# Weight conversion of the first block reordered: joins ahead of the activation, a word pass inside it, the rest behind the copies

## The chip, the cores and the metric

The kernel runs on one core of a Trainium2 chip. The metric is the device time of one execution in microseconds. TensorE (PE) does the matrix products, VectorE (DVE), ScalarE (ACT) and GpSimd (POOL) the elementwise work, and SyncE (SP) issues the DMAs. Each engine takes its instructions strictly in the order in which the program lists them.

## The reference

Three stages follow each other: an attention with a decaying state over 4 batches, 8 heads, 768 steps and 48 features, then two feed-forward layers over 3072 tokens with 384 features and a hidden width of 2048.

```python
for t in range(S):
    state = alpha[:, :, t, :, None] * state + np.einsum('bhd,bhe->bhde', k[:, :, t], v[:, :, t])
    y[:, :, t] = np.einsum('bhd,bhde->bhe', q[:, :, t], state)
x = y.transpose(0, 2, 1, 3).reshape(B * S, H * D)
h = x @ w_in                                        # layer 1
x = (np.maximum(h, 0.0) + alpha * np.minimum(h, 0.0)) @ w_out
h = x @ w_in2                                       # layer 2
g = np.where(h >= 1, h, np.where(h <= -1, 0.0, (h + 1) ** 2 / 4))
out = g @ w_out2
```

The four weight matrices are float64, everything else float32. The kernel needs them as float32.

## The kernel before, in words

The tokens are cut into 24 attention chunks of 128, and for the layers into 6 blocks of 512 (first layer), then 6 blocks of 512 (second). The hidden width is cut into 16 weight chunks of 128. A **step** is one block with one weight chunk: nine hidden products (`emit_h`, L490), the activation (`emit_act`), and the nine products of the step before into the output (`emit_out1`, L523). Step s of the first block uses weight chunk s.

All order is written out by hand: the kernel lists instructions, and every engine takes its own share of the list in that order. The lists `mids` and `ends` hold the pieces of attention that go into a step, `mids` between the hidden and the output products, `ends` behind the output products.

**Activation in layer 1:** ACT scales the hidden product by the leak (L504), DVE takes the maximum (L508), ACT rounds it to `gh` (L513), POOL forms the rest `gl` (L514).

**Weight conversion.** A weight chunk comes in by seven DMAs (`load_w`, L410 to L414) into a staging tile `wst` of which there are three buffers. Its 64-bit words become float32 in two ACT passes (`words_f32`, L420 and L422, "word passes"), and two DVE passes (`join_f32`, L428 and L431, "the join") into a tile `wf`. Then ACT copies it rounded into `wh` (L468, "weight copy") and POOL forms the rest `wl` (L474, "weight pass"). In the first block, step s joins and splits chunk s+2 and does the word passes of chunk s+3. So the first block carries conversion, attention of the next tokens, and its own products at once.

**Attention in the first block.** From step 2 on a chunk takes three steps. Call them A, B and C. In A, PE transposes a part of the next chunk, DVE clamps it (L197), PE transposes the last part (L205), does the output products of the chunk before (L352, L292) and the next state (L324); ACT copies the result (L374, L378), DVE forms its low part (L379, L381) and the state (L336 to L341), and multiplies (L261). In B come the masked products (L311), a scan (L244) and a multiply (L261), in C a scan (L251) and one more transpose (L267).

**The start.** Four attention chunks (c = 0 to 3) run before the first step, on their own, while the first weight chunks load. In c = 2 and 3 their conversion is woven in. There, L363 copies the part of the result that the matmuls with `sel` (L370) spread, and L374 copies the result into the tile `xs` from which the hidden products read.

Of the kernel before, what the change touches and what calls it, by code (L numbers as in the profile page):

```python
# [7 lines left out]
F32 = mybir.dt.float32  # L8
# [14 lines left out]
def kernel(  # L23
# [15 lines left out]
    NT, DM = out.shape  # L39
    DFF = w_in1.shape[1]  # L40
    P = 128
# [3 lines left out]
    NFC = DFF // P  # L45
# [16 lines left out]
    wpool = main.enter_context(tc.tile_pool(name="wpool", bufs=1))  # L62
# [30 lines left out]
    NC0 = NB2 // C  # L93
    spare = iter([f"w{x}{i}" for i in range(NFC - 1, 0, -1) for x in "lh"])
    own = {}

    def spare_tile(key, shape, name):

        if key not in own:
            own[key] = wpool.tile(shape, F32, tag=next(spare), name=name)  # L100
        return own[key]
# [58 lines left out]
    def v_of(c):  # L160

        if c < NC0:
            return spare_tile(("v", c), [P, H, 64], f"v{c}")
        return vt_b[c % 2][:, 0:H * D].rearrange("t (h d) -> t h d", d=D)
# [10 lines left out]
    def load_v(c, eng):  # L175
        b, t0 = c // CPB, (c % CPB) * C
        eng.dma_start(out=v_of(c)[:, :, 0:D], in_=v[b, :, t0:t0 + C, :].rearrange("h t d -> t h d"))
# [239 lines left out]
    def words_f32(lo, hi, t, nbias, part=None):  # L417

        if part != 1:
            nc.scalar.activation(hi.bitcast(F32), t[:, :, 1].bitcast(F32), AF.Copy, scale=2.0 ** -112)  # L420
        if part != 0:
            nc.scalar.activation(lo, t[:, :, 0], AF.Relu, scale=2.0 ** -29, bias=nbias)  # L422
# [16 lines left out]
    def conv_words(layer, fc, part=None):  # L439
        t = stg[layer, fc]  # L440
        if wide:
            w = t.rearrange("p a (n two) -> p (a n) two", two=2)
            words_f32(w[:, :, 0], w[:, :, 1], w, mhalf, part)

    def conv_join(layer, fc, part=None):
        t = stg[layer, fc]
        if wide:
            w = t.rearrange("p a (n two) -> p (a n) two", two=2)
            if part != 1:
                own["f"] = (spare_tile(("f", fc), [P, 2 * DM], "wf") if layer == 0 and fc < 2 else  # L450
                            p1.tile([P, 2 * DM], F32, tag="wf", name="wf"))
            join_f32(own["f"], w[:, :, 0], w[:, :, 1], part)
            if part != 0:
                stg[layer, fc] = own["f"]
        elif part != 0:
            stg[layer, fc] = t.rearrange("p a f -> p (a f)")
# [9 lines left out]
    def split_hi(layer, fc):  # L466
        hi = wpool.tile([P, 2 * DM], F32R, tag=f"wh{fc}", name=f"wh{fc}")
        nc.scalar.copy(out=hi, in_=stg[layer, fc])  # L468
        wt[layer, fc] = [hi, None]

    def split_lo(layer, fc):
        hi = wt[layer, fc][0]
        lo = wpool.tile([P, 2 * DM], F32R, tag=f"wl{fc}", name=f"wl{fc}")
        nc.gpsimd.tensor_sub(out=lo, in0=stg.pop((layer, fc)), in1=hi.bitcast(F32))  # L474
        wt[layer, fc][1] = lo
# [16 lines left out]
                i += 1  # L492
        return hp

    def emit_act(layer, fc, hp, n, parts=1):
        g = p2.tile([P, n], F32, tag="g", name="g", padded_shape=[P, 512])
        gh = p2.tile([P, n], F32R, tag="gh", name="gh", padded_shape=[P, 512])
        gl = p2.tile([P, n], F32R, tag="gl", name="gl", padded_shape=[P, 512])
        cuts = [[t[:, i * n // parts:(i + 1) * n // parts] for t in (hp, g, gh, gl)] for i in range(parts)]
        for x, y, _, _ in cuts:  # L500
            if layer:
                nc.scalar.activation(y, x, AF.Relu, bias=half, scale=0.5)  # L502
            else:
                nc.scalar.activation(y, x, AF.Copy, scale=malpha[:, fc:fc + 1])  # L504
        for x, y, hi, lo in cuts:
            if layer == 0:

                nc.vector.tensor_max(out=y, in0=x, in1=y)  # L508
            else:
                nc.vector.scalar_tensor_tensor(out=y, in0=y, scalar=1.0, in1=y,  # L510
                                               op0=ALU.min, op1=ALU.mult)
                nc.vector.tensor_max(out=y, in0=x, in1=y)  # L512
            nc.scalar.copy(out=hi, in_=y)  # L513
            (nc.gpsimd if parts == 1 else nc.vector).tensor_sub(out=lo, in0=y, in1=hi.bitcast(F32))  # L514
        return gh, gl
# [44 lines left out]
    def xdst(c):  # L560
        j = chunk_blk[c]
        return x_tile(j), c * C - blk[j][1]

    def fetch(c, i=None):

        if c >= NCH:
            return
        if c < NPE:
            for x in (2, 1, 0) if i is None else (i,):
                at_in_pe(c, x, c < NC0)  # L570
            if not i and NC0 + 1 < c + 2 < NPE:
                load_chunk(c + 2, nc.sync)
            if not i and c == NPE - 1:
                nc.gpsimd.memset(natq[:, :, 4 * D - 32:], 1.0)
                load_blocks(NPE)
            return
        for x in (2, 1, 0) if i is None else (i,):
            at_in(c, x)
        if not i and c + 1 < NCH:
            load_blocks(c + 1)  # L580
# [15 lines left out]
    for c in range(NC0, NCH + 1):  # L596
        n = 3 if c < 2 * NC0 else 4
        s = 2 + 3 * (c - NC0) if c < 2 * NC0 else 2 + 3 * NC0 + 4 * (c - 2 * NC0)
# [22 lines left out]
    def run_slots(where, s):  # L621
        for f in where.pop(s, ()):
            f()

    with tc.manual_schedule():
        steps = [(j, fc) for j in range(len(blk)) for fc in range(NFC)]
        gs = {}
        ops_t = {}

        def w1_load(i):  # L630
            if 0 <= i < NFC:
                load_w(0, i, nc.sync)

        def w1_words(i):
            if 0 <= i < NFC:
                conv_words(0, i)

        def w1_join(i):
            if 0 <= i < NFC:
                conv_join(0, i)  # L640

        def w1_split(i):
            if 0 <= i < NFC:
                split_hi(0, i)
                split_lo(0, i)
# [19 lines left out]
                split_hi(1, i)  # L665
                split_lo(1, i)

        def do_h(s):
            j, fc = steps[s]
            layer, t0, n = blk[j]  # L670
            hp = emit_h(layer, fc, xs_t[j], n)
            gs[s] = emit_act(layer, fc, hp, n, 2 if s == len(steps) - 1 else 1)

        def banks(tags, n):

# [80 lines left out]
        for c in range(NC0):  # L756
            i = c - NC0 + 2
            if c < NC0 - 1:
                at_mul(c + 1, "K2", nc.vector)
                at_mul(c + 1, "Q2", nc.gpsimd)  # L760
            at_within(c)
            if c + 2 < NC0:
                fetch(c + 2, 2)
            if c < NC0 - 1:
                at_kt(c + 1)
            if c + 2 < NC0:
                fetch(c + 2, 1)
                fetch(c + 2, 0)
                at_scan(c + 2, "R")
                at_scan(c + 2, "F")  # L770
            w1_join(i)
            at_out(c, xdst(c), True, (lambda: split_hi(0, i)) if i >= 0 else None)
            if c % 2 == 0:
                load_v(NC0 + c // 2, nc.sync)
            if i >= 0:
                split_lo(0, i)
                w1_load(i + 3)
            w1_words(i + 1)
        mps = ps_h.tile([P, NFC], F32, tag="h", name="mps", padded_shape=[P, 512])
        nc.tensor.transpose(out=mps, in_=ma, identity=ident[0:NFC, 0:NFC])  # L780
        nc.scalar.copy(out=malpha, in_=mps)
# [2 lines left out]
        for s in range(len(steps) + SK):  # L784
            if s < len(steps):
                j, fc = steps[s]
                do_h(s)
            run_slots(mids, s)
            if s < NFC:
                w1_join(fc + 2)  # L790
                w1_load(fc + 5)
            if s >= SK:
                do_out(s - SK)
            run_slots(ends, s)
            if s < NFC:
                w1_split(fc + 2)
                w1_words(fc + 3)
            if s < len(steps):
                if j == n1 - 1 and fc == 0:
                    w2_split(-1)  # L800
                if NFC - 2 <= s < (n1 - 1) * NFC:
                    w2_step(s)
                if n1 - 1 <= j < len(blk) - 1:
                    if fc in (8, 10, 12):
                        split_x2(j + 1, (fc - 8) // 2)
                    if fc in (5, 7, 9):
                        load_x2(j + 1, (fc - 5) // 2)
                i = s - (n1 + 1) * NFC
                if i >= 0 and i % 2 == 0 and i // 2 < NFB * NFL:
                    load_flags(i // 2)  # L810
                if i == 0:
                    flag(malpha, 2, 2 * NCH - 1)
                if 0 <= i - 4 < 2 * NFB * NFL:
                    flag(own["al", (i - 4) // 2], i % 2, i - 4)
# [181 lines left out]
```

## Time and profile before

| what | value |
|---|---|
| median of 3 runs | 958.64 us (952.84, 958.64, 958.99) |
| the profiled execution | 952.87 us, its span 951.1 us |
| PE busy over the span | 909.2 us (96%) |
| DVE busy | 493.6 us (52%) |
| ACT busy | 413.8 us (44%) |
| POOL busy | 389.9 us (41%) |
| read from HBM | 66.66 MB |

The shares are means over the whole span, in which the first 158 us (start and first block) and the rest are of two kinds. A time in brackets in a row of a timeline is what the engine sat idle before that instruction, with what ended it.

### The profile page before, as it was taken

Reading aid. Unit: us, or ns where it says so; the run is one execution under the profiler, and the core shown is the slowest. Engines: PE = TensorE matmul, PEld = TensorE weight load, DVE = VectorE, ACT = ScalarE, POOL = GpSimd, SP = SyncE. Lnnn points to the kernel's source line nnn. Section 1 sums busy time; section 2 is a strip of 40 time slices with the busy share of each in tenths; the row PEclk is TensorE's granted clock in tenths of the full one; section 3 lists DMA queues with packets and bytes.
Section 4 is the critical chain, followed back from the end, with each engine's and each line's share of the span. In section 5 each row is a group of like instructions: output and inputs, shape, how many; then the busy total and the mean of one; then the engine's idle time right before and its main releaser. Section 6 shows DMA issues by size and latency. Waiting matters only on the chain.

```text
span 951.1 us, 17365 instructions
## 1 busy us (share of the span) xinstructions
PE 909.2 (96%) x6955; PEld 773.7 (81%) x6955; DVE 493.6 (52%) x675; ACT 413.8 (44%) x668; POOL 389.9 (41%) x310
## 2 busy tenths in 40 slices
PE   6877888999999999999999999999999999999996
PEld 5766667788788788788778889999999999999995
DVE  6588886756666566574312234434335344344332
ACT  2556555444444443444445533346555333333332
POOL 4255454544445444453357743233323332332331
PEclk9899899999999999999999999999999999999999
DMA  9864762674555554462043220122220100100001
GB/s 165 176 139 122 153 121 65 178 179 119 146 146 148 151 129 112 126 175 63 24 162 122 67 67 1 43 81 61 83 67 1 67 1 1 67 1 1 34 1 37
DMA packets 119896, 85.57 MB, mean 90 GB/s; under 512 B 64752, under 2 KB 105472, under 8 KB 119808
## 3 DMA queue, kind: packets, MB, share of 16 engines
q1 hardware_dynamic: 119808, 84.39, 34.7%
q8 instruction: 56, 0.92, 0.4%
q14 instruction: 32, 0.26, 0.1%
HBM read 66.66 MB, written 15.73 MB: 87 GB/s over the span
## 4 chain that ended last, share of the span: by engine, by line
PE 82%; DVE 6%; DMA 5%; SPq 3%; issue 2%; ACT 1%; DVEq 0%; ACTq 0%
PE hp L490 38%; PE y_oo L523 11%; PE y_yy L534 7%; PE y_oo L534 7%; PE y_o L523 5%; PE y_o L534 3%; PE y_at L534 3%; DVE wf L431 2%; DMA wst<-in_moe_w_in_dram 2%; PE w L352 2%; DMA xs<-x 1%; PE w L292 1%; PE w L324 1%; SPq L410 1%; DVE wf L428 1%
## 5 line engine op out<-in xcount | busy, mean ns | idle before, releaser
L514 POOL TENSOR_TENSOR gl<-g,gh 128x512 fp32r<-128x512 f32 x191 | 257.1, 1346 | 486.6 <-ACT gh L513 406.8
L490 PE MATMUL hp<-xs,wh 128*128 128x512 f32 x1152 | 368.3, 401 | 3.1 <-DMA xs<-x 1.3
L490 PEld LDWEIGHTS hp<-xs,wh 128*128 128x128 f32 x1152 | 212.4, 190 | 43.9 <-issue 2.4
L490 PE MATMUL hp<-xs,wl 128*128 128x512 f32 x576 | 227.6, 395 | 0.0
L513 ACT CAST gh<-g 128x512 fp32r<-128x512 f32 (+1 forms) x193 | 119.3, 618 | 226.8 <-DVE g L512 143.9
L510 DVE SCALAR_TENSOR_TENSOR g<-g 128x512 f32<-128x512 f32 (+1 forms) x97 | 67.7, 697 | 207.7 <-ACT g L502 206.3
L490 PEld LDWEIGHTS hp<-xs,wl 128*128 128x128 f32 x576 | 109.3, 190 | 24.1
L508 DVE TENSOR_TENSOR g<-hp,g 128x512 f32<-128x512 f32 x96 | 66.2, 690 | 113.4 <-ACT g L504 112.6
L504 ACT ACTIVATE g<-hp,malpha 128x512 f32<-128x512 f32 x96 | 65.9, 687 | 122.7 <-PE hp L490 121.9
L502 ACT ACTIVATE g<-hp,half 128x512 f32<-128x512 f32 (+1 forms) x97 | 66.5, 686 | 94.0 <-PE hp L490 93.4
L512 DVE TENSOR_TENSOR g<-hp,g 128x512 f32<-128x512 f32 (+1 forms) x97 | 66.5, 686 | 3.4
L523 PE MATMUL y_oo<-gh,wh 128*128 128x512 f32 x192 | 60.2, 395 | 0.0
L523 PE MATMUL y_oo<-gl,wh 128*128 128x512 f32 x192 | 59.7, 392 | 0.4 <-POOL gl L514 0.4
L523 PE MATMUL y_oo<-gh,wl 128*128 128x512 f32 x192 | 59.6, 392 | 0.0
L474 POOL TENSOR_TENSOR wl<-wf,wh 128x768 fp32r<-128x768 f32 x16 | 32.8, 2050 | 30.0 <-ACT wh L468 30.0
L431 DVE SCALAR_TENSOR_TENSOR wf<-wst,wf 128x768 uint32<-128x768 uint32 x32 | 44.4, 1389 | 0.5
L230 DVE STREAM_TRANSPOSE T<-nat 128x512 f32<-128x512 f32 x42 | 43.3, 1084 | 0.0
L523 PEld LDWEIGHTS y_oo<-gl,wh 128*128 128x128 f32 x192 | 36.0, 188 | 8.5 <-POOL gl L514 0.9
L523 PEld LDWEIGHTS y_oo<-gh,wl 128*128 128x128 f32 x192 | 36.1, 188 | 7.7
L523 PEld LDWEIGHTS y_oo<-gh,wh 128*128 128x128 f32 x192 | 35.6, 188 | 7.3
L379 DVE TENSOR_TENSOR xs<-w,xs 128x384 fp32r<-128x384 f32 x24 | 13.4, 558 | 51.1 <-ACT x L378 47.3
L523 PE MATMUL y_o<-gl,wh 128*128 128x512 f32 x96 | 37.7, 393 | 0.0
(123 smaller groups left out, 1384.8 us busy)
## 6 DMA issues: line engine op xcount, KB each, us to landing
wst<-in_moe_w_out_dram SPq DMA_DIRECT2D x32, 384.0 KB, 4.4
wst<-in_moe_w_in_dram SPq DMA_DIRECT2D x16, 384.0 KB, 4.2
w_d<-wf SPq DMA_DIRECT2D x16, 384.0 KB, 2.7
w<-w_d SPq DMA_DIRECT2D x16, 384.0 KB, 3.0
x_d<-ev SPq DMA_DIRECT2D x18, 256.0 KB, 2.5
x2s<-x_d SPq DMA_DIRECT2D x18, 256.0 KB, 3.5
out_dram<-ev SPq DMA_DIRECT2D x24, 192.0 KB, 2.0
al<-in_alpha_dram SPq DMA_DIRECT2D x12, 384.0 KB, 3.3
```

What stands on the lines that cost most here:

```text
L230: nc.vector.transpose(out=tin(c, i).rearrange("f n (j g) -> f n g j", g=4), in_=natq[:, n].rearrange("j n (g f) -> j n g f", g=4)[:, :, :, ...
L431: nc.vector.scalar_tensor_tensor(out=fu, in0=hi, scalar=0x80000000, in1=fu, op0=ALU.bitwise_and, op1=ALU.bitwise_or)
L490: nc.tensor.matmul(out=hp, lhsT=w[:, p, :], rhs=xs[:, x, p, :], start=(i == 0), stop=(i == 3 * ND - 1))
L502: nc.scalar.activation(y, x, AF.Relu, bias=half, scale=0.5)
L504: nc.scalar.activation(y, x, AF.Copy, scale=malpha[:, fc:fc + 1])
L508: nc.vector.tensor_max(out=y, in0=x, in1=y)
L510: nc.vector.scalar_tensor_tensor(out=y, in0=y, scalar=1.0, in1=y, op0=ALU.min, op1=ALU.mult)
L512: nc.vector.tensor_max(out=y, in0=x, in1=y)
L513: nc.scalar.copy(out=hi, in_=y)
L514: (nc.gpsimd if parts == 1 else nc.vector).tensor_sub(out=lo, in0=y, in1=hi.bitcast(F32))
L523: nc.tensor.matmul(out=ops[d], lhsT=w[:, d * P:(d + 1) * P], rhs=g, start=first, stop=last)
L534: nc.tensor.matmul(out=ops[t], lhsT=g[:, t * P:(t + 1) * P], rhs=w, start=first, stop=last)
```

## The change

In the start, the two transposes of a later chunk (`fetch(c + 2, 1)` and `fetch(c + 2, 0)`) go into the chunk's output, behind L363, and the two join passes are parted: the first stays ahead of the output, the second goes behind it. The weight copy leaves the output, and comes last. The loader's call is no longer under `if i >= 0`, and stands ahead of the word passes.

In the first block, the join goes ahead of the hidden products, the first word pass goes into the activation between L504 and the rounding, the second behind the attention's copies, and the weight copy and weight pass behind it. The joined weights of a chunk go into the place of the next chunk's `wl`, where one tile `wf` served most chunks.

```diff
@@ conv_join
             if part != 1:
-                own["f"] = (spare_tile(("f", fc), [P, 2 * DM], "wf") if layer == 0 and fc < 2 else
+
+                own["f"] = (wpool.tile([P, 2 * DM], F32, tag=f"wl{fc + 1}", name="wf")
+                            if layer == 0 and fc + 1 < NFC else
                             p1.tile([P, 2 * DM], F32, tag="wf", name="wf"))
@@ emit_act
+        if mid:
+            mid()
         for x, y, hi, lo in cuts:
@@ the start, for c in range(NC0), i = c - 2
             if c + 2 < NC0:
-                fetch(c + 2, 1)
-                fetch(c + 2, 0)
                 at_scan(c + 2, "R")
                 at_scan(c + 2, "F")
-            w1_join(i)
-            at_out(c, xdst(c), True, (lambda: split_hi(0, i)) if i >= 0 else None)
+            w1_join(i, 0)
+
+            def mid():
+                if c + 2 < NC0:
+                    fetch(c + 2, 1)
+                    fetch(c + 2, 0)
+
+            at_out(c, xdst(c), True, mid)
             if c % 2 == 0:
                 load_v(NC0 + c // 2, nc.sync)
+            w1_join(i, 1)
+            w1_load(i + 3)
+            w1_words(i + 1)
             if i >= 0:
-                split_lo(0, i)
-                w1_load(i + 3)
-            w1_words(i + 1)
+                w1_split(i)
@@ the steps
                 j, fc = steps[s]
-                do_h(s)
+                if j == 0:
+                    w1_join(fc + 2)
+                    w1_load(fc + 5)
+                do_h(s, (lambda: w1_words(fc + 3, 0)) if j == 0 else None)
             run_slots(mids, s)
-            if s < NFC:
-                w1_join(fc + 2)
-                w1_load(fc + 5)
             if s >= SK:
                 do_out(s - SK)
             run_slots(ends, s)
             if s < NFC:
+                w1_words(fc + 3, 1)
                 w1_split(fc + 2)
-                w1_words(fc + 3)
```

How it moves instructions, at three places. The first is SP's queue in the start; `vt0` and `vt1` are v of attention chunks 4 and 5, a tile `wst_` with its number is one load of a weight chunk. Before, wst_605 is chunk 3:

```order
L177 DMA vt0_98<-in_v_dram 128x8x48
L177 DMA vt1_99<-in_v_dram 128x8x48
L410 DMA wst_605<-in_moe_w_in_dram 48x2x256
L410 DMA wst_605<-in_moe_w_in_dram 48x256
L411 DMA wst_605<-in_moe_w_in_dram 16x3x256
```

With the change, where wst_395 is chunk 1, wst_515 chunk 2 and wst_617 chunk 3:

```order
L177 DMA vt0_98<-in_v_dram 128x8x48
L410 DMA wst_395<-in_moe_w_in_dram 48x2x256
...
L414 DMA wst_395<-in_moe_w_out_dram 128x768
L410 DMA wst_515<-in_moe_w_in_dram 48x2x256
...
L414 DMA wst_515<-in_moe_w_out_dram 128x768
L177 DMA vt1_99<-in_v_dram 128x8x48
L410 DMA wst_617<-in_moe_w_in_dram 48x2x256
```

Two loads of seven DMAs each are new there; the loads of chunks 1 and 2 that stood earlier in the queue (wst_187 and wst_197) stand there still.

The second is ACT's queue at the end of the start, from the fourth chunk's transposes on. Before (wst_187 is the first load of chunk 1):

```order
L269 COPY KT_542<-kt_537 128x512
L363 COPY y3_381<-w_477 128x128
L468 CAST wh0_592<-wf_544 128x768
L374 CAST xs_343<-w_477 128x3x128
L420 ACTIVATE wst_187<-wst_187 128x768
L422 ACTIVATE wst_187<-wst_187,mhalf_96 128x768
L363 COPY y3_494<-w_571 128x128
L468 CAST wh1_669<-wf_641 128x768
L374 CAST xs_343<-w_571 128x3x128
```

With the change:

```order
L269 COPY KT_558<-kt_553 128x512
L363 COPY y3_369<-w_473 128x128
L374 CAST xs_331<-w_473 128x3x128
L420 ACTIVATE wst_395<-wst_395 128x768
L422 ACTIVATE wst_395<-wst_395,mhalf_96 128x768
L470 CAST wh0_627<-wf_560 128x768
L363 COPY y3_490<-w_586 128x128
L374 CAST xs_331<-w_586 128x3x128
```

The weight copy moved behind the word passes, and the word passes of chunk 1 read wst_395, the new load.

The third is DVE's queue in one step A of the first block. Before (scan of C, then maximum, clamp, join, low part of the result, state, multiply):

```order
L251 SCALAR_TENSOR_TENSOR F_1002<-T1_104,zfw_90 128x516
L508 TENSOR_TENSOR g_1021<-hp_1011,g_1021 128x512
L197 TENSOR_SCALAR T0_103<-tr_1028 128x4x128
L428 SCALAR_TENSOR_TENSOR wf_1034<-wst_834 128x768
L431 SCALAR_TENSOR_TENSOR wf_1034<-wst_834,wf_1034 128x768
L379 TENSOR_TENSOR xs_1063<-w_851,xs_1063 128x3x128
L381 TENSOR_TENSOR x3_1098<-w_851,x3_1098 128x128
L339 TENSOR_TENSOR bd1_101<-w_851,bd0_100 128x4x48
L261 TENSOR_TENSOR Q2_1110<-T1_104,F_1002 128x512
```

With the change (the maximum is now line 512):

```order
L251 SCALAR_TENSOR_TENSOR F_1019<-T1_104,zfw_90 128x516
L428 SCALAR_TENSOR_TENSOR wf_1027<-wst_827 128x768
L431 SCALAR_TENSOR_TENSOR wf_1027<-wst_827,wf_1027 128x768
L512 TENSOR_TENSOR g_1048<-hp_1038,g_1048 128x512
L197 TENSOR_SCALAR T0_103<-tr_1056 128x4x128
L379 TENSOR_TENSOR xs_1080<-w_868,xs_1080 128x3x128
L381 TENSOR_TENSOR x3_1115<-w_868,x3_1115 128x128
L339 TENSOR_TENSOR bd1_101<-w_868,bd0_100 128x4x48
L261 TENSOR_TENSOR Q2_1127<-T1_104,F_1019 128x512
```

The join moved from behind the clamp to ahead of the maximum; between the clamp and L379 nothing stands any more.

## Rows read from the trace of the kernel before

**Rows 1.** Table by stretches: stretch, its length, busy time per engine, clock, DMA.

```profile
63.17:151.35 88.18, 73.36 (x710) 58.40 (x708) 77.20 (x77) 50.58 (x75) 45.08 (x27) 0.92 0.54 118
158.00:945.00 787.00, 782.33 (x5476) 670.60 (x5474) 371.76 (x524) 333.10 (x544) 317.45 (x235) 1.00 0.28 81
```

**Rows 2.** Timeline of SP in the start: start, duration, engine, line, operation, count.

```profile
38.53 2.11 SPq L177 DMA_DIRECT2D vt<-in_v_dram  x2
40.75 2.01 SPq L410 DMA_DIRECT2D wst<-in_moe_w_in_dram  x2
...
44.67 0.42 SPq L414 DMA_DIRECT2D wst<-in_moe_w_out_dram  x1
```

**Rows 3.** DMA issues of the first 60 us: median from issue to landing.

```profile
wst<-in_moe_w_out_dram SPq DMA_DIRECT2D x6, 384.0 KB, 3.6
```

**Rows 4.** Landings of all DMAs into wst, first 60 us.

```profile
DMA to landing us min/median/max: 2.0/3.3/4.7
```

**Rows 5.** Timeline of ACT in the start, from the word passes of chunk 1.

```profile
37.78 0.91 ACT L420 ACTIVATE wst<-wst 128x768 f32<-128x768 f32 x1
38.58 1.00 ACT L422 ACTIVATE wst<-wst,mhalf 128x768 uint32<-128x768 uint32 x1
40.17 0.27 ACT L363 COPY y<-w 128x128 f32<-128x128 f32 x1 [0.59 <-PE w L292]
41.60 0.83 ACT L468 CAST wh<-wf 128x768 fp32r<-128x768 f32 x1 [1.17 <-DVE wf L431]
42.34 0.47 ACT L374 CAST xs<-w 128x384 fp32r<-128x384 f32 x1
```

**Rows 6.** Timeline of PE at the end of the start.

```profile
40.49 1.55 PE L370 MATMUL w<-y,sel 128*128 128x64 f32 x12 [0.43 <-ACT y L363]
...
42.86 1.39 PE L490 MATMUL hp<-xs,wh 128*128 128x512 f32 x2 [0.66 <-ACT xs L374]
```

**Rows 7.** Timeline of DVE from the end of a step C into A.

```profile
81.68 1.23 DVE L251 TENSOR_TENSOR_SCAN F<-T,zfw 128x516 f32<-128x516 f32 x1
84.70 0.69 DVE L508 TENSOR_TENSOR g<-hp,g 128x512 f32<-128x512 f32 x1 [1.79 <-ACT g L504]
85.31 0.68 DVE L197 TENSOR_SCALAR T<-tr 128x512 f32<-128x512 f32 x1
85.91 0.95 DVE L428 SCALAR_TENSOR_TENSOR wf<-wst 128x768 uint32<-128x768 uint32 x1
86.89 1.91 DVE L431 SCALAR_TENSOR_TENSOR wf<-wst,wf 128x768 uint32<-128x768 uint32 x1
89.29 0.56 DVE L379 TENSOR_TENSOR xs<-w,xs 128x384 fp32r<-128x384 f32 x1 [0.49 <-ACT x L378]
...
90.23 2.26 DVE L261 TENSOR_TENSOR Q<-T,F 128x512 f32<-128x512 f32 x1
```

**Rows 8.** Timeline of DVE, the same places one period later.

```profile
106.80 0.69 DVE L508 TENSOR_TENSOR g<-hp,g 128x512 f32<-128x512 f32 x1 [1.77 <-ACT g L504]
...
112.33 0.56 DVE L379 TENSOR_TENSOR xs<-w,xs 128x384 fp32r<-128x384 f32 x1 [1.43 <-ACT x L378]
...
113.66 1.86 DVE L261 TENSOR_TENSOR Q<-T,F 128x512 f32<-128x512 f32 x1
```

**Rows 9.** Timeline of POOL beside rows 7 and just after.

```profile
86.18 1.81 POOL L514 TENSOR_TENSOR gl<-g,gh 128x512 fp32r<-128x512 f32 x1 [1.62 <-issue]
...
90.07 1.87 POOL L474 TENSOR_TENSOR wl<-wf,wh 128x768 fp32r<-128x768 f32 x1 [0.89 <-ACT wh L468]
94.13 1.28 POOL L514 TENSOR_TENSOR gl<-g,gh 128x512 fp32r<-128x512 f32 x1 [2.19 <-ACT gh L513]
```

**Rows 10.** Timeline of DVE: a multiply as a POOL instruction (30.48 to 31.76) ends.

```profile
31.54 0.77 DVE L261 TENSOR_TENSOR K<-T,R 128x512 f32<-128x512 f32 x1
```

**Rows 11.** Timeline of PE in the step A of rows 7.

```profile
86.05 0.66 PE L205 MATMUL tr<-ident,nat 128*128 128x128 f32 x4 [2.69 <-DVE T L197]
...
88.51 1.22 PE L490 MATMUL hp<-xs,wh 128*128 128x512 f32 x2
```

More of the change, by code (lines that the diff above doesn't have):

```diff
@@ L493, in emit_h, with emit_act @@
         return hp
-    def emit_act(layer, fc, hp, n, parts=1):
+    def emit_act(layer, fc, hp, n, parts=1, mid=None):
         g = p2.tile([P, n], F32, tag="g", name="g", padded_shape=[P, 512])
@@ L632, in w1_load, with w1_words, w1_join @@
                 load_w(0, i, nc.sync)
-        def w1_words(i):
+        def w1_words(i, part=None):
             if 0 <= i < NFC:
-                conv_words(0, i)
-        def w1_join(i):
+                conv_words(0, i, part)
+        def w1_join(i, part=None):
             if 0 <= i < NFC:
-                conv_join(0, i)
+                conv_join(0, i, part)
         def w1_split(i):
@@ L666, in w2_split, with do_h @@
                 split_lo(1, i)
-        def do_h(s):
+        def do_h(s, mid=None):
             j, fc = steps[s]
@@ L671, in do_h @@
             hp = emit_h(layer, fc, xs_t[j], n)
-            gs[s] = emit_act(layer, fc, hp, n, 2 if s == len(steps) - 1 else 1)
+            gs[s] = emit_act(layer, fc, hp, n, 2 if s == len(steps) - 1 else 1, mid)
         def banks(tags, n):
```

## Prediction

> **What bounds the kernel now.** I read the table by stretches first [rows 1]. From 158 us on TensorE (PE) is busy 782.33 of 787.00 us at granted clock 1.00, so whatever the first 158 us lose or win is carried to the end unchanged. The change touches only what runs before that. From the start of the maximum (L508) of step 2 to that of step 14, 63.17 to 151.35, PE is busy only 73.36 of 88.18 us and VectorE (DVE) 77.20: there DVE is the engine that is nearly full. Four periods of three steps lie in it, 88.18 / 4 = 22.05 us each.
>
> Next I read one period on DVE [rows 7]. A chunk's first step (A) runs maximum 84.70, clamp 85.31, join 85.91 and 86.89, and then waits: the low part of the attention output, L379, starts only at 89.29, since it needs a chain that the clamp released. That chain is on PE: the transposes of L205 sat idle 2.69 us for the clamp [rows 11], then came the chunk's output matmuls and the copies on ScalarE (ACT). Clamp to L379 is 3.98 us, 3.38 of them after the clamp's 0.60; one period later 112.33 - 107.41 is 4.92, as the maximum at 106.80 [rows 8] plus 0.61 gives the clamp. Today the join fills that gap, and the idle time left is 0.49 and 1.43 us. The other idle time is before A's maximum: 1.79 and 1.77 us, because ACT's L504 stands behind the weight copy and two word passes.
>
> Last I read the start, ahead of the first hidden matmul at 42.86 [rows 6]: ACT's word passes of chunk 1 at 37.78 [rows 5], and SP's queue [rows 2].
>
> **The change, part by part.**
>
> *Loads.* In the start the call of the loader loses its condition and stands ahead of the word passes. The order shows 14 more DMAs on SP: chunks 1 and 2 are loaded twice, and the word passes read the second copies (wst_395 and wst_515). The first copies are never read. The second load of chunk 1 stands directly behind the first of two v loads. Those two take 2.11 us together from 38.53 [rows 2], so it starts at about 39.6. Chunk 3's load, which stands there today, takes from 40.75 to 45.09 to issue, 4.34 us; so the last DMA of the new one is issued at about 43.9, and lands 3.6 us later by the median of that tensor [rows 3]: 47.5. With the bounds for all loads of that tile, 2.0 and 4.7 us [rows 4], 45.9 to 48.6. I take 47.5, as the 3.6 is of the same tensor and queue.
>
> The word passes of chunk 1, at 37.78 today, then wait 9.7 us. ACT runs in order, and behind them stand the weight copy of chunk 0, the copy L363 and the cast L374 of the last chunk, without which the first hidden matmul cannot start. From the landing: two word passes 0.80 + 0.90, weight copy 0.75, L363 0.30 [rows 5], the sel matmuls 1.55 [rows 6], L374 0.50: 4.8 us, so 52.3 in place of 42.86, +9.4 us. Of this the first steps give something back: in step 0 the two join passes (0.96 each) no longer lie behind its maximum. Between 0 and 1.9 us I take 0.6, since DVE is not alone in setting the pace of those steps. Net +8.8; by the bounds +5.9 to +10.5. The second load of chunk 2 waits for chunk 0's join, which is over before SP comes to it at 43.9; it is issued by 48 and landed by 51.7, ahead of its passes at about 52.3: nothing. Load 3 stands behind it and a v load, lands at about 56, and its first use, in step 0 behind L506, comes at about 56 too: nothing to 1, I take nothing. Later loads have two steps of time: nothing.
>
> *Transposes into the chunk's output, the weight copy out of it.* These move ahead of and behind work that ACT waits for anyway, and all of it ends before 47.5: nothing. The joined weights in the later tiles' places free the single wf buffer; no DVE join in [rows 7] starts late for it (85.91 follows the clamp by 0.60): nothing.
>
> *The order in the steps.* DVE now runs join, maximum, clamp in A. Gained at most: the idle time in the four periods, 88.18 - 77.20 = 11.0 us [rows 1]. Lost: the join no longer fills the gap behind the clamp. I add up one period in the new order with the rows' lengths. DVE's own work: six join passes of 0.96, three maxima and one clamp of 0.60, L379 up to the multiply 1.33 (112.33 to 113.66), two multiplies of 0.77, the mask 0.60, two scans of 1.23 with 0.2 for the reciprocal: 14.3 us. The gap behind the clamp: 3.1 (the rows say 3.4, and 4.3 at a slower PE; part of POOL's wait falls into it).
>
> Then collisions with GpSimd (POOL). A multiply takes 0.77 with POOL all but at rest [rows 10] and 2.26 beside POOL's weight pass, which ran 90.07 to 91.94 [rows 9]; it ended 0.55 after POOL did. The second join pass took 1.91 instead of 0.96 in the same way beside gl (86.18 to 87.99). So a DVE operation with both inputs in SBUF waits till the POOL instruction is over. In the new order the weight pass (1.83) follows ACT's last instruction of the step, when the next join is up; it holds one join pass of each step, and gl (1.27) [rows 9] holds one multiply and one join: 3 x 1.83 + 2 x 1.27 = 8.0 us. Today the weight pass partly runs in DVE's idle time, and collisions are about 5.9. Period: 14.3 + 3.1 + 8.0 = 25.4. The same addition for the old order gives 22.9 (the trace: 106.80 - 84.70 = 22.1), so I use the difference, 2.5 us. Two periods are whole (steps 5 to 11); in the first the chunk has no L379, in the last the joins run out: 0 to 0.5 together. Sum +5.5; bounds -11.0 (all idle time gone, no gap) and +15 (four whole periods with the 4.3 us gap: 4 x 3.7).
>
> The Trainium skill, page "SBUF — State Buffer", section "SBUF: two separate sides", calls the port pair of VectorE and GpSimd an exclusive lock, held for a whole instruction, which an operation with two SBUF inputs needs too. It speaks against this change: by it the collisions are 8.0 and the block +5.5; were they as long as today's, about +1. The trace agrees, by the 2.26 us.
>
> *Sum.* +8.8 + 5.5 = +14.3 us. The profiled execution took 952.87 us (span 951.1), so 967.2 on its level. It is the lower of two levels among the runs: 952.84 against 958.64 and 958.99. On the median's level it is 958.64 + 14.3 = 972.9. Two of three runs were on the upper one, so I take **971 us**.
>
> **Rivals.**
>
> 1. *The load stalls, the orders break even* (period 22 us as today). For: the bookkeeping's 2.5 us is one tenth of a period, and it overstates the old order by 0.8. Then +8.8: 967 on the median's level. Chance 0.17, on the border of no change.
> 2. *The joins first do what they promise*: A's maximum waits no more, and the gap is filled by something I do not see. Block -9 to -11 with the stall +8.8: 957 to 959. Against: nothing but L379 stands behind the clamp on DVE. Chance 0.13.
> 3. *Faster*: the second load of chunk 1 lands before the pass wants it, and the idle time goes too. Place: ACT's L420 of chunk 1; price 9.4 us; it decides if the landing is before 39 us. Then 958.64 - 11 = 948. For: v loads ahead are small. Against: SP does not reach it before 39.6. Chance 0.10.
> 4. *The stall is hidden* (that part of the change is not what the order says), the period is longer: 958.64 + 5.5 = 964. Chance 0.05.
> 5. *PE's clock*. After the wait of 2.69 us [rows 11] the first two hidden matmuls took 1.22 us, and the granted clock of the four periods is 0.92 [rows 1], between the two levels of 1.2 and 2.4 GHz. Longer waits put more matmuls at the lower one, and the chain behind the clamp is then 0.9 us longer (4.92 against 3.98), in each of four periods, the start's matmuls 2 us: 971 + 5.6 = 977. Chance 0.07. The Trainium skill, "TensorE: Matmul & The Clock Gate", section "What's actually happening", says that the array's clock is low by default and activity releases it; by that rule the time is 977.
>
> **The numbers.** Forecast 0.48 and its branch 5 0.07, with a small part of 1 (0.03): slower by over 1% (above 968.2), 0.58. Within 1%, which is about what a measurement of this kernel can tell from no change: the rest of 1, with 2 and 4, 0.32. Faster by over 1%: 0.10. Range 957 to 981: it takes in 1, 2 and 4, the lower level of the forecast (967), and 5; outside lie 3 and a block worse than its upper bound.
>
> **What would show it.** In the profile after: ACT idle some 9 us before L420 of the start, released by a DMA into wst; the first hidden matmul at 51 to 53 us; 14 more issues from in_moe_w_in and in_moe_w_out, 1.6 MB more read; DVE idle 3 to 4 us before L379 in each A step and none before the maximum; maximum to maximum 24 to 25.5 us. If L420 starts before 40 us, the load term is wrong; if the period is under 22, the order term is. A first hidden matmul at 52 with a total below 960 would mean that block 1 gained what I say it loses.

## The result, and the profile after

The changed kernel takes 967.41 us, median of 7 runs (965.05 to 971.39), against 958.64 (952.65 to 959.62, 7 runs) for the one before: ratio 1.0111, 95% interval 1.0078 to 1.0143. It is slower, by about 1%; the two medians stand 8.8 us apart. Its profiled execution took 967.41 us too (span 965.7), 14.5 more than the 952.87 of before's profile.

The table by stretches; first the maximum (now L512) of step 2 to that of step 14, then ten microseconds of the start, then the rest (columns as in [rows 1]):

```profile
74.56:165.84 91.28, 75.34 (x709) 58.59 (x708) 72.58 (x77) 49.37 (x75) 44.23 (x27) 0.91 0.50 110
42.00:52.00 10.00, 1.04 (x5) 1.04 (x6) 0.96 (x1) 2.61 (x4) 1.18 (x1) 0.50 0.84 206
160.00:945.00 785.00, 779.98 (x5534) 667.66 (x5532) 372.79 (x522) 332.93 (x543) 322.44 (x239) 1.00 0.29 81
```

Set against [rows 1]: step 2's maximum comes at 74.56 instead of 63.17, so 11.4 us are lost ahead of it. The stretch up to step 14 takes 91.28 instead of 88.18, 3.1 more; in it DVE is busy 4.6 less, and idle 18.7 instead of 11.0. Behind it nothing differs: from step 15's maximum (172.24, before 157.75) to the end it is 793.5 us, before 793.4. And in the start there are ten microseconds with little work on any engine. This is what ends them. ACT, timeline (answers to [rows 5]):

```profile
34.07 0.48 ACT L374 CAST xs<-w 128x384 fp32r<-128x384 f32 x1 [1.71 <-PE w L370]
48.29 0.88 ACT L420 ACTIVATE wst<-wst 128x768 f32<-128x768 f32 x1 [13.74 <-DMA wst<-in_moe_w_in_dram]
49.07 0.95 ACT L422 ACTIVATE wst<-wst,mhalf 128x768 uint32<-128x768 uint32 x1
49.93 0.81 ACT L470 CAST wh<-wf 128x768 fp32r<-128x768 f32 x1
50.65 0.26 ACT L363 COPY y<-w 128x128 f32<-128x128 f32 x1
53.82 0.48 ACT L374 CAST xs<-w 128x384 fp32r<-128x384 f32 x1 [2.91 <-PE w L370]
```

SP's queue, where the new load of chunk 1 is issued (answers to [rows 2]):

```profile
39.67 1.34 SPq L177 DMA_DIRECT2D vt<-in_v_dram  x1
41.06 1.60 SPq L410 DMA_DIRECT2D wst<-in_moe_w_in_dram  x2
...
44.58 0.42 SPq L414 DMA_DIRECT2D wst<-in_moe_w_out_dram  x1
```

And PE, which then starts the first block (answers to [rows 6]):

```profile
50.96 2.83 PE L370 MATMUL w<-y,sel 128*128 128x64 f32 x12 [13.37 <-ACT y L363]
...
54.35 1.39 PE L492 MATMUL hp<-xs,wh 128*128 128x512 f32 x2 [0.35 <-ACT xs L374]
```

ACT is ready at 34.6 and sits still for 13.74 us until the second copy of chunk 1 has come in, the last DMA of which SP issues from 44.58 to 45.00. L363 and L374 of the last chunk stand behind it, so the first hidden matmul starts at 54.35, not 42.86.

In the block, DVE through one step A and on into the next (answers to [rows 7, 8]):

```profile
92.12 1.19 DVE L428 SCALAR_TENSOR_TENSOR wf<-wst 128x768 uint32<-128x768 uint32 x1 [0.72 <-ACT wst L422]
93.34 2.47 DVE L431 SCALAR_TENSOR_TENSOR wf<-wst,wf 128x768 uint32<-128x768 uint32 x1
95.73 0.68 DVE L512 TENSOR_TENSOR g<-hp,g 128x512 f32<-128x512 f32 x1
96.33 0.68 DVE L197 TENSOR_SCALAR T<-tr 128x512 f32<-128x512 f32 x1
101.21 0.56 DVE L379 TENSOR_TENSOR xs<-w,xs 128x384 fp32r<-128x384 f32 x1 [4.20 <-ACT x L378]
...
102.15 0.68 DVE L261 TENSOR_TENSOR Q<-T,F 128x512 f32<-128x512 f32 x1
...
103.73 2.49 DVE L431 SCALAR_TENSOR_TENSOR wf<-wst,wf 128x768 uint32<-128x768 uint32 x1
...
107.66 0.69 DVE L311 TENSOR_TENSOR A<-w,mask 128x512 f32<-128x512 f32 x1 [0.83 <-PE w L306]
108.27 1.68 DVE L244 TENSOR_TENSOR_SCAN R<-T,zrev 128x516 f32<-128x516 f32 x1
110.05 2.10 DVE L261 TENSOR_TENSOR K<-T,R 128x512 f32<-128x512 f32 x1
...
116.70 1.18 DVE L428 SCALAR_TENSOR_TENSOR wf<-wst 128x768 uint32<-128x768 uint32 x1 [0.72 <-DMA wst<-in_moe_w_in_dram]
117.91 2.47 DVE L431 SCALAR_TENSOR_TENSOR wf<-wst,wf 128x768 uint32<-128x768 uint32 x1
120.31 0.68 DVE L512 TENSOR_TENSOR g<-hp,g 128x512 f32<-128x512 f32 x1
...
125.82 0.56 DVE L379 TENSOR_TENSOR xs<-w,xs 128x384 fp32r<-128x384 f32 x1 [4.24 <-ACT x L378]
```

The idle time ahead of the maximum is gone, and in its place stand 4.20 us behind the clamp, with nothing to fill them. Maximum to maximum is 24.58 us (120.31 - 95.73), before 22.10. The wait of 0.72 is put down to a DMA, but ACT's word pass on the same tile, L422, ended only at 116.66, so it is that pass which the join waited for. POOL beside the two slow join passes (answers to [rows 9]):

```profile
92.95 2.04 POOL L476 TENSOR_TENSOR wl<-wf,wh 128x768 fp32r<-128x768 f32 x1 [0.46 <-ACT wh L470]
...
102.94 2.47 POOL L476 TENSOR_TENSOR wl<-wf,wh 128x768 fp32r<-128x768 f32 x1 [2.66 <-ACT wh L470]
```

and PE in this step A, where the chain behind the clamp runs (answers to [rows 11]):

```profile
97.07 1.11 PE L205 MATMUL tr<-ident,nat 128*128 128x128 f32 x4 [3.09 <-DVE T L197]
```

The four transposes take 1.11 us here and 0.66 in [rows 11]: PE runs that chain at a lower clock. That is not new with the change, as the next step A of the kernel before shows:

```profile
108.15 1.12 PE L205 MATMUL tr<-ident,nat 128*128 128x128 f32 x4 [2.67 <-DVE T L197]
```

### The profile page after: what moved, and what is told of

The parts are those of the page before. It is cut to its first block, busy times and chain, and to the rows that moved or that the text cites. A ratio compares the mean times of both kernels' runs of the same rounds, so it can differ in the third digit from the quotient of the medians.

```text
span 965.7 us, 17384 instructions
## 1 busy us (share of the span) xinstructions
PE 910.0 (94%) x6955; PEld 772.2 (80%) x6955; DVE 492.1 (51%) x675; ACT 412.8 (43%) x668; POOL 390.8 (40%) x310
## 4 chain that ended last, share of the span: by engine, by line
PE 77%; DVE 7%; DMA 7%; SPq 5%; issue 2%; ACT 2%; DVEq 0%; ACTq 0%
PE hp L492 36%; PE y_oo L527 10%; PE y_yy L538 7%; PE y_oo L538 7%; PE y_o L527 5%; PE y_o L538 3%; PE y_at L538 3%; DVE wf L431 3%; DVE wf L428 2%; DMA wst<-in_moe_w_in_dram 2%; DMA wst<-in_moe_w_out_dram 2%; SPq L410 2%; SPq L172 1%; PE w L352 1%; DMA xs<-x 1%
## 5 line engine op out<-in xcount | busy, mean ns | idle before, releaser
L518 POOL TENSOR_TENSOR gl<-g,gh 128x512 fp32r<-128x512 f32 x191 | 259.8, 1360 | 495.1 <-ACT gh L517 439.2
L506 ACT ACTIVATE g<-hp,malpha 128x512 f32<-128x512 f32 x96 | 66.2, 689 | 128.7 <-PE hp L492 128.7
L512 DVE TENSOR_TENSOR g<-hp,g 128x512 f32<-128x512 f32 x96 | 66.2, 689 | 100.9 <-ACT g L506 100.1
L504 ACT ACTIVATE g<-hp,half 128x512 f32<-128x512 f32 (+1 forms) x97 | 66.5, 686 | 94.0 <-PE hp L492 94.0
L428 DVE SCALAR_TENSOR_TENSOR wf<-wst 128x768 uint32<-128x768 uint32 x32 | 39.5, 1236 | 18.0 <-ACT wst L422 16.5
L379 DVE TENSOR_TENSOR xs<-w,xs 128x384 fp32r<-128x384 f32 x24 | 13.4, 558 | 62.1 <-ACT x L378 55.6
L431 DVE SCALAR_TENSOR_TENSOR wf<-wst,wf 128x768 uint32<-128x768 uint32 x32 | 41.9, 1311 | 0.5
L205 PE MATMUL tr<-ident,nat 128*128 128x128 f32 x120 | 22.4, 323 | 21.0 <-DVE T L197 10.7
```

Source lines behind the costliest of these rows:

```text
L428: nc.vector.scalar_tensor_tensor(out=fu, in0=hi, scalar=3, in1=lo, op0=ALU.logical_shift_left, op1=ALU.bitwise_or)
L431: nc.vector.scalar_tensor_tensor(out=fu, in0=hi, scalar=0x80000000, in1=fu, op0=ALU.bitwise_and, op1=ALU.bitwise_or)
```

## The experiments

The theory: the second loads cost the start some 9 us or more, the order of the joins costs the block 3 to 5. The rivals: the order is a gain that the load hides, or the second loads cost as DMA traffic and not as a wait. "Step 16" below is the first ACT instruction of the second block's activation (L504 before, L506 after), at 163.1 in the profile of before and 177.5 after. Each ratio is to runs of the kernel before that were taken beside the run itself, with medians of 954.86 and 956.38 us rather than 958.64; so the ratios can be set against each other, and the times only roughly.

**The change without the second loads.**

```diff
-            w1_load(i + 3)
+            if i >= 0:
+                w1_load(i + 3)
```

> The changed kernel with the loader's call in the start again under its condition, so that chunks 1 and 2 are loaded once; all else as changed. Theory (the second loads stall ACT, then DVE's order costs a little): ACT's first word pass of chunk 1 starts at 34 to 35 us in place of 48.3, the first hidden matmul at 40 to 41 in place of 54.35, and the time falls by 12 to 14.5 us against the changed kernel, to about the time of the kernel before (within 4 us). Rival (the loss is in the order of the steps, the start only idles where it would have waited later): less than 5 us are won.

958.16 us, ratio to the kernel before 1.0041 (1.0026 to 1.0057); its profile 954.14, which is 13.3 less than after's. By the ratios the second loads cost 0.7%, some 7 us, and by the medians 9.3; the 12 to 14.5 that were expected came only in the profile. ACT's first word pass of chunk 1 started at 36.10, not at 34 to 35, and the first hidden matmul at 43.07, not at 40 to 41: the product with `sel` took 2.82 us, as in the changed kernel, though PE had hardly waited for it:

```profile
39.68 2.82 PE L370 MATMUL w<-y,sel 128*128 128x64 f32 x12 [0.43 <-ACT y L363]
```

So the second loads are most of the loss, and the rest of the change is still no gain.

**The kernel before with the second loads alone.**

```diff
             if i >= 0:
                 split_lo(0, i)
-                w1_load(i + 3)
+            w1_load(i + 3)
```

> The kernel before, with the second loads of chunks 1 and 2 as the one change. Theory: the first hidden matmul moves from 42.86 to 52 to 55 us and the time rises by 9 to 12 us. Rival (the loads are hidden, since the block is bound by DVE and catches up): under 4 us.

963.78 us, 1.0107 (1.0081 to 1.0133): one moved line gives the whole change's ratio. The first hidden matmul came at 53.78, as expected. ACT's timeline at the pass, then the stretch from step 2 to 14:

```profile
48.46 0.88 ACT L420 ACTIVATE wst<-wst 128x768 f32<-128x768 f32 x1 [10.72 <-DMA wst<-in_moe_w_in_dram]
```

```profile
74.48:162.64 88.16, 75.17 (x711) 59.71 (x709) 77.19 (x77) 50.65 (x75) 44.38 (x27) 0.90 0.52 118
```

The landing is the same as after, within 0.2 us; the wait is 3.0 shorter since ACT comes to it later. The block takes 88.16, as before (88.18), and step 16 is 11.3 later.

**The same loads into tiles that nothing reads.** The 14 DMAs of the run above stay, at the same places, and the word passes read the first copies.

```diff
+        again = (layer, fc) in stg
+        if again:
+            t0, t1 = [spare_tile(("wsx", fc, x), [P, wn * DM], "wsx").bitcast(U32) for x in range(2)]
...
-        stg[layer, fc] = t
+        if not again:
+            stg[layer, fc] = t
```

> The kernel before with the 14 additional DMAs of e2_reload_only at the same places of SP's queue, but into tiles that nothing reads, so that the word passes of chunks 1 and 2 read the first copies. Theory (what costs is ACT waiting for the second copies; the transfers themselves only push chunk 3's load back by some 8 us): the first hidden matmul stays at 42 to 44 us, ACT waits 2 to 6 us for chunk 3 in step 0, and the time rises by 2 to 6 us. Rival (the transfers and the queue are the cost, whoever reads them): 9 us or more, as in e2_reload_only.

954.81 us, 1.0028 (0.9994 to 1.0063): 2.7 us, the low end of what was expected, with no change at all inside the interval. The first hidden matmul came at 41.85, step 16 at 163.7, 0.7 later than before; what is left is a wait in step 0, for chunk 3, whose load now stands behind 14 DMAs:

```profile
55.79 0.88 ACT L426 ACTIVATE wst<-wst 128x768 f32<-128x768 f32 x1 [4.06 <-DMA wst<-in_moe_w_in_dram]
```

That wait puts step 2's maximum back by 3.1 us (66.23), and by step 14 all but 0.6 of it is made up. So in the trace the loads as traffic cost 0.7 us up to step 16, and in the time nothing that can be told from noise; the wait for the second copies costs the rest of the 11.3. The traffic rival falls.

**The new order of the steps alone** (the changed kernel with the start of before: its loop from `fetch(c + 2, 1)` to `w1_words(i + 1)` as it was).

```diff
-            w1_join(i, 0)
...
-            w1_join(i, 1)
-            w1_load(i + 3)
-            w1_words(i + 1)
             if i >= 0:
-                w1_split(i)
+                split_lo(0, i)
+                w1_load(i + 3)
+            w1_words(i + 1)
```

> The kernel before, with the order in the steps of the first block (and the places of the joined weights) of the changed one, and the start of the kernel before. Theory (the join no longer fills DVE's gap behind the clamp, and meets POOL's weight pass): maximum to maximum of two A steps 24 to 25.5 us for steps 5 to 11, where it was 22.1 and 23.4; the time rises by 2 to 6 us. Rival (joins first pay, and the block of the changed kernel was longer only as its start was late and the clock low): the time falls by 3 to 10 us.

957.82 us, 1.0037 (1.0014 to 1.0061). The stretch from step 2 to 14 takes 91.36, its whole periods 24.56 and 25.02, and the gap is there without any second load (DVE, step A; one period later it is 4.24):

```profile
90.78 0.56 DVE L379 TENSOR_TENSOR xs<-w,xs 128x384 fp32r<-128x384 f32 x1 [4.20 <-ACT x L378]
```

The order is a loss of its own, 3.2 us in the block; that it is a hidden gain falls. Step 16 is 4.2 later, but 1.0 of that stands ahead of step 2, in a start that is the one of before. There the `sel` product took 2.82 us, and 1.55 in [rows 6], behind the same wait of 0.43:

```profile
40.54 2.82 PE L370 MATMUL w<-y,sel 128*128 128x64 f32 x12 [0.43 <-ACT y L363]
```

**The new start alone** (before's block, the change's start, the loader's call under its condition).

```diff
-            w1_join(i)
-            at_out(c, xdst(c), True, (lambda: split_hi(0, i)) if i >= 0 else None)
+            w1_join(i, 0)
...
+            at_out(c, xdst(c), True, mid)
...
+            w1_join(i, 1)
...
+            if i >= 0:
+                w1_split(i)
```

> The kernel before, with the start of the changed one (transposes behind the copy, parted join, weight copy last) without the second loads. Theory from the trace of the changed kernel, where the result of the third chunk was cast at 34.07 us and not 37.41: the first hidden matmul 2.5 to 3.5 us earlier, the time 2 to 3.5 us lower. Rival (what I predicted: these moves are worth nothing, as the loads from HBM set the pace of the start): within 1 us.

953.03 us, 0.9997 (0.9974 to 1.0019). In the trace it gains: first hidden matmul at 41.17 instead of 42.86, step 16 2.8 earlier. In the time that can't be told from nothing. The stretch from step 2 to 14 takes 86.80.

**POOL's weight pass done twice** (on the change without second loads; chunks 2 to 15).

```diff
+        if layer == 0 and fc >= 2:
+            nc.gpsimd.tensor_sub(out=lo, in0=stg[layer, fc], in1=hi.bitcast(F32))
         nc.gpsimd.tensor_sub(out=lo, in0=stg.pop((layer, fc)), in1=hi.bitcast(F32))
```

> The changed kernel without the second loads, where POOL does the weight pass of weight chunks 2 to 15 twice over (the same subtraction into the same place), 14 passes of 1.83 us more. Theory (DVE's two-input operations wait for a whole POOL instruction): most of the additional passes meet a join, a multiply or a scan and add their length to DVE's path, so the steps 0 to 15 are 12 to 26 us longer, and the time rises by as much against e1_no_reload. Rival (POOL has idle time, two thirds of the stretch, and DVE is slowed by something else): under 4 us.

967.71 us, 1.0143 (1.0079 to 1.0207). Step 15's maximum comes at 171.59, 12.4 later than without (159.16), for 14 passes more: the low end of what was expected, and far above the rival. In the time it is 1.0% more than the 1.0041 of the run without second loads, some 10 us, which is less than the 12 that were expected. The stretch from step 2 to 14, here and in that run:

```profile
64.13:165.12 100.99, 76.41 (x706) 56.80 (x705) 83.34 (x76) 49.11 (x74) 71.69 (x39) 0.93 0.45 99
63.11:152.76 89.65, 71.59 (x690) 54.98 (x682) 72.67 (x77) 48.92 (x74) 44.03 (x27) 0.94 0.50 112
```

Of the 11.3 us more, 10.7 are busy time of DVE, whose work is the same. POOL, then DVE at a step A:

```profile
85.95 2.05 POOL L477 TENSOR_TENSOR wl<-wf,wh 128x768 fp32r<-128x768 f32 x1 [0.47 <-ACT wh L470]
88.08 2.41 POOL L478 TENSOR_TENSOR wl<-wf,wh 128x768 fp32r<-128x768 f32 x1
```

```profile
86.34 2.48 DVE L431 SCALAR_TENSOR_TENSOR wf<-wst,wf 128x768 uint32<-128x768 uint32 x1
88.74 0.68 DVE L514 TENSOR_TENSOR g<-hp,g 128x512 f32<-128x512 f32 x1
...
99.87 1.93 DVE L244 TENSOR_TENSOR_SCAN R<-T,zrev 128x516 f32<-128x516 f32 x1
```

The join pass, both inputs in SBUF, takes 2.48 and ends 0.8 behind the first POOL pass; a maximum, with `hp` in PSUM, takes its usual 0.68 in the middle of the second. The scan waits like the join (1.93; 1.23 in [rows 7]).

**The join back behind the clamp, in the steps A alone** (on the change without second loads).

```diff
+                late = j == 0 and fc >= 2 and fc % 3 == 2
-                if j == 0:
+                if j == 0 and not late:
                     w1_join(fc + 2)
...
+            if s < NFC and late:
+                w1_join(fc + 2)
+                w1_load(fc + 5)
```

> The changed kernel without the second loads (as e1_no_reload), and in each step A of the first block (2, 5, 8, 11) the join again behind the clamp; in the other steps it stays ahead of the maximum. Theory (the gap behind the clamp is what the order loses): DVE's idle time before L379 in A falls from 4.2 us to under 1.5, the steps 2 to 14 take 84 to 87 us from maximum to maximum (e1_no_reload 89.7), the time is 3 to 6 us under e1_no_reload. Rival (the collisions with POOL set the period, wherever the join stands): within 1 us of e1_no_reload.

953.27 us, 0.9966 (0.9935 to 0.9997). From step 2 to 14 it takes 83.70 (84 to 87 was expected), against 89.65 with joins first. The gap behind the clamp is gone in most periods; a wait ahead of A's maximum is back:

```profile
83.79 0.69 DVE L512 TENSOR_TENSOR g<-hp,g 128x512 f32<-128x512 f32 x1 [2.04 <-ACT g L506]
```

**Joins behind the clamp in every step; in the block only ACT's order as changed** (on the change without second loads, so the start stays as changed, and so do the places of the joined weights).

```diff
-                if j == 0:
-                    w1_join(fc + 2)
-                    w1_load(fc + 5)
                 do_h(s, (lambda: w1_words(fc + 3, 0)) if j == 0 else None)
             run_slots(mids, s)
+            if s < NFC:
+                w1_join(fc + 2)
+                w1_load(fc + 5)
```

> The changed kernel without the second loads, with DVE's order in the steps as before (maximum, clamp, join), so that only ACT's new order is left (a word pass in the activation, the other behind the copies, weight copy last). Theory: the 1.8 us in which DVE waited for ACT before A's maximum go, and the gap behind the clamp stays filled: the steps 2 to 14 take 83 to 86 us (88.2 before, 86.8 in e3_start_only), the time is 3 to 6 us under e1_no_reload and 2 to 4 under e3_start_only. Rival (the weight copy, last on ACT, makes the weight pass late and it then holds DVE's multiplies longer): no faster than e3_start_only.

**946.71 us, 0.9902 (0.987 to 0.9934)**: faster than both kernels, and by more than was expected. The stretch from step 2 to 14, where 83 to 86 us were expected, DVE in a step A, and POOL's weight pass of that step:

```profile
61.77:142.63 80.86, 71.82 (x716) 56.87 (x714) 72.96 (x77) 50.64 (x75) 45.63 (x28) 0.96 0.58 130
```

```profile
81.82 0.69 DVE L512 TENSOR_TENSOR g<-hp,g 128x512 f32<-128x512 f32 x1 [0.39 <-ACT g L506]
82.43 0.68 DVE L197 TENSOR_SCALAR T<-tr 128x512 f32<-128x512 f32 x1
83.03 0.95 DVE L428 SCALAR_TENSOR_TENSOR wf<-wst 128x768 uint32<-128x768 uint32 x1
84.01 1.92 DVE L431 SCALAR_TENSOR_TENSOR wf<-wst,wf 128x768 uint32<-128x768 uint32 x1
85.96 0.56 DVE L379 TENSOR_TENSOR xs<-w,xs 128x384 fp32r<-128x384 f32 x1
...
86.90 0.68 DVE L261 TENSOR_TENSOR Q<-T,F 128x512 f32<-128x512 f32 x1
```

```profile
87.69 1.85 POOL L476 TENSOR_TENSOR wl<-wf,wh 128x768 fp32r<-128x768 f32 x1 [1.38 <-ACT wh L470]
```

The join fills the gap, and the maximum waits 0.39 instead of 1.79, since on ACT no word pass stands between the weight copy and L506 any more. But idle time is the smaller part of the gain: DVE's idle time in the stretch falls by 3.1 us (7.9 from 11.0), and its busy time by 4.2 (72.96 from 77.20) for the same 77 instructions. The multiply behind L379 takes 0.68 instead of 2.26 [rows 7], as POOL's weight pass now starts behind it. The run of the new start alone, which has the same start and the old block, has 86.80 against the 80.86 here. The granted clock of the stretch is 0.96 (0.92 before); the clock does not explain the gain, as the run above had 1.00 and took 83.70.

## Why the prediction came out, step by step

The time was foreseen within 4 us and the sum in the traces (+14.3) within 0.3, but this is partly luck: the two terms were off by 2.6 and 2.4 us, in opposite directions.

**What bounds it: held.** All of the 14.5 us is there at step 14 (165.84 - 151.35), and it is carried to the end.

**The second loads: right mechanism, +8.8 foreseen, +11.4 measured** (step 2's maximum). SP had issued the last DMA of chunk 1 at 45.00 (43.9 was said), the pass began at 48.29 (47.5): 0.8 of the miss. ACT sat idle for 13.74 us and not some 9, as the new start brings it there earlier; that costs nothing. From the landing to the first hidden matmul it took 6.06 us, not 4.8, and 1.28 of the difference is the `sel` product, 2.83 instead of 1.55. The 0.6 us to be given back in step 0 was 0.1. The granted clock from 42 to 52 us was 0.50, the level of 1.2 GHz, and PE was busy in it for 1.04 of 10 us. This is the rival on PE's clock, in the start. The Trainium skill, "TensorE: Matmul & The Clock Gate", section "What's actually happening", says that the clock is low by default and released by activity, and this row agrees. But the product took 2.82 behind a wait of 0.43 in the run without second loads, and in the run of the new order alone, whose start is the one of before. So the 1.28 us are not shown to come from the second loads.

**The start's reordering "nothing": wrong as a price, nearly right in the sum.** ACT's cast of the third chunk comes at 34.07, 3.3 earlier than before (37.41), and the new start alone gains 2.8 us up to step 16. In the change ACT then only waits longer for the same landing: the second loads alone (+11.3 at step 16) and the order alone (+3.2 in the block; its 1.0 in the start is the `sel` product, which the 11.3 holds already) make 14.5, and the whole change has 14.5. So by this sum none of the 2.8 came through: the fixed landing hid it, which is the reason that the prediction gave.

**The order in the steps: right sign, +5.5 foreseen, +3.1 measured, and mostly not from the term that I named.** From one A's maximum to the next it was 21.53, 22.10, 23.43 and 21.12 us, and is 21.17, 24.58, 24.91 and 20.62. The two whole periods (steps 5 to 11) cost 2.48 and 1.48, where I said 2.5 each; the first and the last, for which I added 0 to 0.5, gave back 0.86. In the first whole period the number is right, and its parts are not:

| term | before (84.70 to 106.80) | foreseen | measured (95.73 to 120.31) |
|---|---|---|---|
| idle behind the clamp | 0.49 | 3.1 | 4.20 |
| idle ahead of A's maximum | 1.79 | 0 | 0 |
| collisions with POOL | 5.85 | 8.0 | 5.05 |
| new waits (mask for PE, join for a word pass) | 0 | 0 | 0.83 + 0.72 |
| DVE's own work, the rest | 13.97 | 14.3 | 13.78 |
| whole period | 22.10 | 25.4 | 24.58 |

The foreseen rise is 2.5, as the prediction's addition gave 22.9 for the old order. Of it, 2.1 were collisions (8.0 against 5.9) and 0.4 idle time (3.1 against the 2.75 of a mean period). In this period the collisions fell by 0.8 and the idle time rose by 3.5. The whole stretch says the same: DVE idle 7.7 us more, busy 4.6 less; 1.9 of the 4.6 is one join fewer in it (11, before 12), so the rest, some 2.7, is shorter collisions. What the order costs is the unfilled gap, as the prediction also said, and not more collisions.

I let every POOL weight pass hold a DVE operation for all its 1.83 us, but they only overlap in part: the five slow ones lost 1.53, 0.46, 1.33, 0.22 and 1.51 us. The prediction gave two cases, 8.0 by the lock or as long as today, and the trace is below both. Of the 5.85 of today, 2.44 are the join pass and the multiply of [rows 7]; the rest is this:

```profile
94.23 1.99 DVE L431 SCALAR_TENSOR_TENSOR wf<-wst,wf 128x768 uint32<-128x768 uint32 x1
...
98.06 2.11 DVE L261 TENSOR_TENSOR K<-T,R 128x512 f32<-128x512 f32 x1
...
101.68 2.00 DVE L431 SCALAR_TENSOR_TENSOR wf<-wst,wf 128x768 uint32<-128x768 uint32 x1
```

That an operation waits for the whole of another one, as the Trainium skill has it in "SBUF — State Buffer", section "SBUF: two separate sides", agrees with the doubled weight pass: the join took 2.48 instead of 0.96.

The gap was 1.1 larger than said, as PE's chain ran at the lower clock (1.11 against 0.66 for the transposes), which was the price that the rival on the clock named. In the run without second loads the gap was 3.07, nearly the 3.1 of the prediction, in a step A where the transposes took 0.66, and 4.23 in one where they took 1.12.

**The level.** On the profile's own level 967.2 was foreseen, and 967.41 came. I moved it to 971 because two of three runs of before lay at about 959. By the medians the change costs 8.8 us, by the ratio 10.6 (0.0111 x 958.64), by the traces 14.5. That shift was the step that did not hold: the changed kernel's median lies where its profile lies. By the ratio the result is over the 1% that I had set as the bound of a change; by the medians, 0.9%, it stays under it.

**The rivals.** "The orders break even" named 967 us, and 967.41 came, so the time cannot tell it from the forecast; it falls by its reason (the new order alone is 1.0037 with an interval above 1, and the block is 3.1 longer). "The joins first pay" falls (block +3.2, not -9 to -11). "Faster" falls, as SP did not reach the new load before 41.06. "The stall is hidden" falls with the 13.74 us. The clock's price was paid in part, 1.28 us in the start and 1.1 behind the clamp of a period, but the kernel before pays the latter too in its next period, and the granted clock of the stretch only went from 0.92 to 0.91; so 977 did not come.

**What the prediction did not see:** a part of the change is a gain. With the start as changed in all three, the block takes 86.80 us with the old order, 80.86 with ACT's new order, and 89.65 with ACT's and DVE's: a gain of 5.9 and a loss of 8.8. I had charged both as one edit. I had named DVE's idle time as all that could be won, and did not see that another order on ACT moves POOL's weight pass, and with it the collisions: most of the gain is there.

## What to carry to other kernels

When several edits touch one loop, price each engine's order by itself: here one change holds a gain (word passes moved out of the way of ACT's scaling, which also moves POOL's weight pass) and a larger loss (DVE's gap filler moved away). Before moving work off a spot, look at which wait it was covering; the join cost next to nothing behind the clamp, where DVE had to wait for L379 anyway. Here a load that was issued again cost little as traffic, and in the traces some 11 us where an engine that runs in order had to read the second copy.

## What was not expected of the hardware

The six blocks of the second layer, the same instructions in every kernel here, take different times in different executions, with PE busy throughout and the granted clock at 1.00. From step 95 to step 191, in the profile of after, then of the run with only ACT's order changed:

```profile
554.70:953.30 398.60, 398.31 (x2012) 361.42 (x2011) 160.52 (x218) 161.89 (x272) 129.28 (x99) 1.00 0.11 34
```

```profile
531.90:936.80 404.90, 404.62 (x2012) 365.62 (x2011) 160.49 (x218) 161.88 (x272) 128.76 (x99) 1.00 0.10 34
```

That is 66.4 us a block against 67.5, and 6.3 us in all; DVE and ACT are busy as long in both. It is about the distance between the two levels of before's runs (952.7 and 959), whose profile has 66.4 a block; whether the upper runs are of this kind, no trace shows. It can also put a profile's time and a median some us apart: the new order alone took 960.2 in its profile (67.0 a block) and 957.82 in the median. What makes the difference stays open.
